# New orders for all engines, and another stretch of late landings in the planner, in an attention and squared-ReLU kernel

## The chip, the core and the metric

The kernel runs on one core of a Trainium2 chip. The metric is the device time of one execution in microseconds: 356.66 us before, the median of three runs (356.45 to 357.16). All times are microseconds (us) unless marked ns. The engines are TensorE (PE, its weight loads PEld), VectorE (DVE), ScalarE (ACT), GpSimd (POOL) and SyncE (SP).

## The reference

Inputs are float32: `q`, `k`, `v` of shape (8 batches, 8 heads, 576 positions, 64), a table of 32 buckets x 8 heads, and two weight matrices.

```python
scores = q @ k.T / 8 + bias_table[bucket(|i - j|)]      # bucket: exact below 16, then logarithmic, 31 from 128 on
attn   = softmax(scores)                                # per batch and head, 576 x 576
x      = (attn @ v), heads put side by side             # 4608 tokens x 512
h      = maximum(x @ w_in, 0)                           # w_in 512 x 2048
out    = (h * h) @ w_out                                # w_out 2048 x 512, float32 result
```

## The kernel before

**Attention.** Two heads make a pair; there are 32 pairs, four to a batch. The softmax is taken without its maximum: the exponential of the scaled scores is multiplied by the exponential of the bias, which is one constant outside a band round the diagonal, so that only the band is multiplied (`tt`, L807, on DVE). The exponential of the table is built at the start: six pieces of 16 small matmuls each on PE (`t_mm`, L531), evacuated by ACT (L543) or DVE (L545).

A pair's q and k are loaded by POOL's queue with a cast to fp16 (L439), into one of five places `qs`/`ks`; for batches 0 and 1 PE transposes them (`tr`, L1096), and ACT (L793) or DVE (L795) copies them out of PSUM into `qt`/`kt`. Later batches are transposed by DMAs that SP issues (L1079). The first pair's q and k come in as float32 by SP and ACT and are cast (L657 on ACT, L659 on DVE). The last 64 keys of both heads share one matmul; for it two small copies per pair put them on a block diagonal in `kz` (L1123, POOL or DVE).

Batch 0 is worked in two halves of its queries (L1013 to L1037), four pairs each. For one pair and half: two score groups of four matmuls (L961), each into two PSUM banks and out through one exponential of 128x1024 on ACT (L1013); one matmul for the last keys (L1028) and its exponential (L1037); band products on DVE; the values (`pv`, L833 and L840) on PE, which need all four value tiles and both tails of the batch; a reciprocal and a product that normalise (L854, L859). Values of batches 0 and 1 are loaded by token tile, one DMA for each 128 tokens (`va`) and two for the last 64 (`vm`). Later pairs have one score group per 128 keys, with an exponential of 128x1024 each (L1143).

**Feed-forward.** Tokens go in nine groups of 512. Group 0 runs its first layer in halves as soon as half of batch 0 is done (L1585; ReLU L1596 on ACT or L1598 on DVE; square L454 on ACT or L456 on DVE). The other first layers (L1633, or L1512 with seven products in place of eight) and second layers (L1342, seven products for eight, with sums of weights L1272 and of activations L1297 on DVE) fill PE between the attention's matmuls from some 54 us to the end.

**What sets the order.** Every operation has a number, counted in the order in which the Python code makes it. `TURNS` (L69) is a table with, for each engine, the numbers in the order in which that engine runs them; where an operation may run on ACT or DVE (or DVE or POOL), the list that holds its number decides. `Plan.schedule` walks these lists with planned durations and planned landings of loads; it doesn't change the order on an engine, but it settles which PSUM bank or buffer an operation takes and how the engines' instructions are interleaved in the program. In it, `SLOW` says between which planned times a DMA lands later, and by how much:

```python
late = SLOW[2] if e == "DMA" and SLOW[0] < at < SLOW[1] else 0.0
```

Of the kernel before, what the change touches and what calls it, by code (L numbers as in the profile page):

```python
# [70 lines left out]
12 15 21 17 19 537 23 535 541 543 25 559 563 571 547 553 573 561 549 555 575 583 587 585 568 597 595 599 580 622  # L71
626 592 604 624 609 607 628 667 669 735 733 637 611 641 683 634 613 652 686 654 639 680 643 656 762 619 658 747
749 677 649 664 760 789 787 814 816 741 739 692 673 671 689 745 820 766 710 707 743 701 770 704 713 768 774 822
716 695 698 719 776 772 755 757 722 756 830 795 782 784 854 858 797 783 675 863 824 867 801 799 793 874 878 803
828 883 887 836 809 826 892 896 811 810 837 838 903 907 841 843 914 847 845 918 952 944 950 851 849 875 942 948
979 871 884 880 911 973 971 977 889 946 864 860 975 855 900 1008 981 1002 893 1004 904 925 1010 958 1000 959 960
1006 1035 987 988 989 922 915 1016 1029 1037 1017 1078 1079 1018 1161 1033 1081 1082 1031 1159 1039 1089 1093
1186 1192 1045 1047 1046 1098 1221 1163 1194 1102 1190 1107 1111 1196 1188 1157 1118 1122 1225 1223 1217 1129
1133 1215 1202 1165 1108 1115 1204 1219 1203 1119 1167 1254 1090 1067 1060 1062 1069 1130 1126 1137 1072 1086
1075 1099 1104 1064 1095 1140 1231 1250 1244 1232 1248 1233 1293 1376 1294 1380 1173 1252 1174 1296 1175 1246  # L80
1372 1297 1304 1401 1378 1260 1308 1261 1262 1313 1374 1407 1382 1317 1322 1403 1432 1440 1326 1333 1438 1436
1430 1337 1434 1344 1388 1409 1348 1405 1389 1390 1446 1585 1591 1448 1447 1587 1305 1593 1411 1583 1341 1319
1352 1589 1417 1459 1277 1275 1419 1418 1282 1279 1301 1284 1463 1334 1330 1645 1290 1310 1465 1651 1461 1287
1345 1314 1641 1467 1469 1323 1355 1649 1599 1600 1601 1504 1505 1475 1670 1672 1477 1476 1507 1508 1674 1515
1678 1614 1519 1524 1528 1680 1647 1618 1533 1537 1643 1612 1657 1544 1545 1534 1676 1548 1566 1616 1541 1488
1659 1486 1493 1658 1490 1555 1556 1498 1525 1495 1521 1622 1854 1563 1856 1501 1552 1530 1512 1516 1559 1628
1686 1620 1687 1688 1715 1716 1827 1630 1629 1718 1719 1802 1800 1862 1726 1730 1852 1860 1823 1735 1739 1744
1796 1804 1794 1748 1755 1798 1759 1727 1858 1810 1825 1766 1741 1697 1699 1811 1704 1763 1706 1812 1732 1701
1709 1770 1883 1889 1887 1712 1777 1752 1891 1829 1831 1774 1767 1868 1881 1833 1723 1736 1870 1756 1885 1869
1745 2044 1839 2038 1840 1841 1930 1931 1897 2075 2046 1898 1933 1899 2048 2073 1934 1941 2077 2009 2011 1945  # L90
1950 2067 2017 2040 1954 1959 2042 2013 1963 2069 2015 2054 1970 1967 2056 2055 1912 2071 1974 1960 1916 1914
2096 2019 1947 1919 2102 2098 1942 1938 2100 1978 2104 2083 1924 1921 2084 1992 1989 1927 2085 1971 1982 1956
2025 2112 2106 2026 1951 2027 2113 2114 2185 2186 1981 1985 2188 2189 2193 2194 2196 2197 2199 2200 2204 2123
2125 2130 2147 2145 2127 2152 2132 2205 2135 2138 2154 2167 2157 2176 2213 2149 2160 2212 2169 2174 2216 2209
2245 2179 2238 2240 2223 2171 2182 2247 2256 2220 2296 2298 2258 2250 2253 2242 2314 2315 2260 2263 2265 2317
2276 2274 2318 2268 2281 2271 2322 2323 2325 2300 2278 2283 2326 2303 2305 2286 2328 2289 2329 2308 2333 2311
# [3 lines left out]
6 2 10 13 52 16 18 20 24 536 544 560 572 564 574 562 550 576 584 588 586 598 596 600 627 623 625 610 629 608 638  # L100
642 612 614 653 655 640 681 644 657 682 659 748 750 679 761 790 817 742 740 672 690 746 821 767 712 744 702 709
771 714 769 823 715 696 775 697 777 773 699 723 700 831 796 859 798 825 868 802 800 794 804 829 827 842 848 953
945 951 943 949 980 885 877 886 974 978 972 947 861 976 856 866 901 982 1009 1005 1003 905 1011 1001 906 927
1007 1036 923 916 1030 1038 1080 1162 1034 1032 1040 1160 1187 1193 1222 1195 1191 1164 1197 1158 1189 1226 1218
1224 1216 1166 1220 1117 1120 1168 1255 1121 1061 1131 1127 1128 1071 1139 1074 1088 1100 1065 1101 1096 1141
1251 1245 1249 1377 1295 1381 1253 1247 1373 1402 1379 1375 1383 1408 1404 1441 1433 1439 1437 1435 1431 1410
1406 1586 1592 1588 1306 1412 1307 1584 1342 1594 1321 1590 1354 1276 1460 1280 1281 1464 1303 1335 1336 1646
1331 1311 1652 1462 1466 1347 1642 1468 1470 1356 1325 1650 1506 1671 1673 1675 1679 1615 1681 1648 1619 1644
1613 1546 1547 1677 1567 1617 1542 1543 1487 1491 1492 1558 1526 1527 1522 1623 1855 1857 1553 1554 1531 1532
# [1633 lines left out]
```

## Time and profile before

| what | value |
|---|---|
| median of three runs | 356.66 us |
| the profiled execution's own time | 356.16 us |
| its span, first to last instruction | 354.2 us |
| PE busy | 346.2 us (98%) |
| DVE, ACT, POOL busy | 304.0, 270.0, 164.4 us |
| mean granted TensorE clock | 0.995 |
| DMA | 44.38 MB, mean 125 GB/s |

The page lists busy time by engine, then the span in 40 slices, DMA queues, the chain of work that ended last, and the costliest groups of instructions. Matmuls are pipelined, so that a busy PE is not PE at its peak. A timeline row gives start, duration, engine, line, operation, written tile, read tile, shape and count, and in brackets the idle time before it with what ended it. A row of waits gives the sum, the number and the longest.

### The profile page before, as it was taken

The numbers are of one execution on the slowest core, as the hardware profiler recorded it, in microseconds if no ns is written. First come the engines' busy times: TensorE is split into PE (matmuls) and PEld (weight loads), VectorE is DVE, ScalarE is ACT, GpSimd is POOL, SyncE is SP. The second block draws the span as 40 slices with busy tenths as digits, with TensorE's granted clock in tenths as the row PEclk, the third lists the DMA queues.
The fourth block names the chain that finished last, engine by engine and source line by source line (L and its number), as shares of the span: only waits on it lengthen the run. The fifth ranks groups of instructions, "written<-read, shape, count | busy, mean of one in ns | idle before, by whom it ended". The sixth has DMA issues, their size and how long they took to land.

```text
span 354.2 us, 10890 instructions
## 1 busy us (share of the span) xinstructions
PE 346.2 (98%) x4456; PEld 259.3 (73%) x4456; DVE 304.0 (86%) x624; ACT 270.0 (76%) x400; POOL 164.4 (46%) x282
## 2 busy tenths in 40 slices
PE   8799999999999999999999999999999999999996
PEld 7577777854687657778776757765777788878885
DVE  5899999779986989787999797789968998999993
ACT  5898996379978788789968684889797941999820
POOL 8857669589969759596856632300000000000000
PEclk9899999999999999999999999999999999999999
DMA  9999999999999999999999978632522042000023
GB/s 170 184 185 174 205 170 144 126 189 175 153 186 165 193 145 143 171 195 171 153 127 172 165 58 150 138 78 67 78 51 78 2 59 89 31 31 32 17 75 120
DMA packets 161378, 44.38 MB, mean 125 GB/s; under 512 B 144688, under 2 KB 161328, under 8 KB 161328
## 3 DMA queue, kind: packets, MB, share of 16 engines
q0 software_dynamic: 74144, 14.53, 50.3%
q1 hardware_dynamic: 86928, 28.86, 47.1%
q8 instruction: 35, 0.57, 0.7%
q10 hardware_dynamic: 256, 0.30, 0.3%
q14 instruction: 15, 0.12, 0.1%
HBM read 36.94 MB, written 9.44 MB: 131 GB/s over the span
## 4 chain that ended last, share of the span: by engine, by line
PE 83%; ACT 8%; DVE 4%; DMA 2%; issue 1%; POOL 1%; ACTq 0%; POOLq 0%
PE bank L1342 32%; PE bank L1633 17%; PE bank L1512 10%; PE bank L899 9%; PE bank L961 7%; ACT pt L1143 3%; DMA ks<-in_k_dram 2%; ACT pt L1013 2%; PE bank L1156 2%; PE bank L968 1%; PE bank L883 1%; PE bank L1585 1%; ACT g L454 1%; PE bank L840 1%; DVE g L456 1%
## 5 line engine op out<-in xcount | busy, mean ns | idle before, releaser
L1143 ACT ACTIVATE pt<-bank 128x1024 f16<-128x1024 f32 x112 | 110.2, 1030 | 13.3 <-PE bank L961 12.9
L1633 PE MATMUL bank<-xt,w_in_sb 128*128 128x512 f16 (+4 forms) x416 | 77.9, 330 | 0.2 <-DVE x L922 0.2
L807 DVE TENSOR_TENSOR pt<-pt,tb_sb 128x512 f16<-128x512 f16 (+3 forms) x108 | 60.5, 574 | 12.9 <-ACT pt L1143 8.6
L439 POOL DMA_DIRECT2D qs<-in_q_dram x79 | 55.8, 712 | 15.2 <-DMA qt<-qs 8.5
L1342 PEld LDWEIGHTS <-g 128*128 128x128 f16 x576 | 54.8, 98 | 8.7 <-issue 2.3
L439 POOL DMA_DIRECT2D ks<-in_k_dram x79 | 55.6, 709 | 2.5 <-issue 1.0
L1633 PEld LDWEIGHTS <-w_in_sb 128*128 128x128 f16 x416 | 36.9, 98 | 26.4 <-issue 3.3
L1342 PEld LDWEIGHTS <-s 128*128 128x128 f16 x432 | 40.8, 98 | 8.5 <-issue 3.6
L961 PE MATMUL bank<-qt,kt 64*128 64x512 f16 (+1 forms) x288 | 42.0, 361 | 0.2
L899 PEld LDWEIGHTS <-pt 128*128 128x128 f16 x1120 | 37.6, 97 | 5.0 <-issue 2.6
L1370 DVE SCALAR_TENSOR_TENSOR y<-bank,y 128x512 f32<-128x512 f32 (+1 forms) x48 | 31.9, 664 | 10.5 <-PE bank L1342 9.8
L899 PE MATMUL bank<-va,pt 128*128 128x65 f16 x1120 | 40.3, 193 | 0.4 <-DVE pt L807 0.4
L1342 PE MATMUL bank<-w_out_sb,s 128*128 128x256 f16 x288 | 36.1, 273 | 0.0
L1342 PE MATMUL bank<-wt,g 128*128 128x256 f16 x288 | 35.9, 273 | 0.0
L1123 POOL COPY kz<-kt 64x64 f16<-64x64 f16 x59 | 18.2, 309 | 37.3 <-DMA kt<-ks 28.2
L1342 PE MATMUL bank<-w_out_sb,g 128*128 128x256 f16 x288 | 35.1, 273 | 0.0
L454 ACT ACTIVATE g<-rt 128x512 f16<-128x512 f16 x49 | 30.9, 639 | 2.0 <-DVE rt L1664 1.4
L1662 ACT ACTIVATE rt<-bank 128x512 f16<-128x512 f32 x42 | 24.8, 596 | 7.6 <-PE bank L1633 7.3
L1664 DVE TENSOR_SCALAR rt<-bank 128x512 f16<-128x512 f32 x38 | 26.0, 687 | 4.2 <-PE bank L1633 3.1
L727 POOL CAST va<-f 128x512 f16<-128x512 f32 x24 | 16.2, 678 | 22.2 <-issue 14.0
L1297 DVE TENSOR_TENSOR s<-g,s 128x1024 f16<-128x1024 f16 x36 | 24.6, 691 | 0.0
L922 DVE TENSOR_TENSOR x<-bank,r 128x640 f16<-128x640 f32 x28 | 22.9, 819 | 0.4
(120 smaller groups left out, 559.8 us busy)
## 6 DMA issues: line engine op xcount, KB each, us to landing
out_dram<-y SPq DMA_DIRECT2D x34, 256.0 KB, 2.4
f<-in_v_dram SPq DMA_DIRECT2D x24, 256.0 KB, 4.8
qs<-in_q_dram POOLq DMA_DIRECT2D x48, 64.0 KB, 4.9
ks<-in_k_dram POOLq DMA_DIRECT2D x48, 64.0 KB, 4.9
w_in_sb<-in_moe_w_in_dram POOLq DMA_DIRECT2D x4, 512.0 KB, 7.1
w_out_sb<-in_moe_w_out_dram POOLq DMA_DIRECT2D x4, 512.0 KB, 10.4
va<-in_v_dram POOLq DMA_DIRECT2D x8, 128.0 KB, 6.5
qs<-in_q_dram POOLq DMA_DIRECT2D x7, 144.0 KB, 6.2
```

The lines of the kernel that those rows point to most:

```text
L439: lambda: io(eng.dma_start(out=out_(), in_=in_())),
L454: io(nc.scalar.activation(out=out_, in_=src, func=SQUAREF))
L807: io(nc.vector.tensor_tensor(out=a, in0=a, in1=t, op=MULT))
L899: nc.tensor.matmul(of_head(st, e)[:, ts(i, 65)], pt[:, c : c + 128], va[:, jt, 2 * hp + e, 0:65], start=False, stop=(jt == 3), skip_group_ ...
L961: nc.tensor.matmul(banks[i][e], kt[rw[e], ts(jt, 128)], qt[rw[e], ds(q0, n)], start=True, stop=True)
L1143: nc.scalar.activation(out=p5(pts[pb.slot])[:, jt, :, 0:512], in_=in_two(st), func=EXPF, scale=SCALE)
L1342: nc.tensor.matmul(home[bf.slot][:, ts(s_, HALF)], left(c, s_), right(c), start=(c == 0 and (s_ == 0 or apart) and (own or i not in before ...
L1370: nc.vector.scalar_tensor_tensor(out=dst, in0=ps, scalar=OSC, in1=ys[y[plus].slot][:, cs], op0=MULT, op1=mybir.AluOpType.add,)
L1512: nc.tensor.matmul(ps()[:, ds(HALF * f + a, z - a)], left()[:, kk, ts(f, 128)], right(a, z)[:, kk, :], start=(first_ and f == 0 and a == 0 ...
L1633: nc.tensor.matmul(g_ps[bank.slot][:, a:z], w_in_sb[:, kk, ts(nt, 128)], xt_sb[:, kk, c : c + z - a], start=(kk == 0), stop=(kk == 3),)
L1662: io(nc.scalar.activation(out=rts[rb.slot], in_=g_ps[bank.slot], func=RELUF))
L1664: io(nc.vector.tensor_scalar_max(out=rts[rb.slot], in0=g_ps[bank.slot], scalar1=0.0))
```

## The change

Two things are edited. `SLOW` goes from 800 ns late between 12.0 and 23.0 us of the plan to 550 ns late between 8.4 and 9.8 us. All five lists of `TURNS` are replaced. The set of operations is the same, and so are their sizes; 133 operations run on another engine than before (most are ReLUs, squares and copies out of PSUM, about as many from ACT to DVE as the other way), and loads stand in another order in POOL's list.

```diff
 TURNS = {
     "PE": """
-12 15 21 17 19 537 23 535 541 543 25 559 563 571 547 553 573 561 549 555 575 583 587 585 568 597 595 599 580 622
+12 15 19 25 23 537 541 535 549 547 559 543 21 587 17 573 563 583 571 575 561 555 553 585 568 595 599 597 580 622
...
     "POOL": """
-53 65 55 73 57 67 71 69 75 59 539 61 63 545 103 77 540 87 99 81 551 79 107 85 97 83 109 89 738 737 111 105 93 95
+53 67 65 55 75 61 69 71 59 57 539 73 551 63 87 545 103 77 81 99 79 107 558 85 109 89 97 737 738 83 105 111 113
...
-SLOW = 12000.0, 23000.0, 800.0
+SLOW = 8400.0, 9800.0, 550.0
```

All line numbers after the table are one lower in the changed kernel, whose table takes one line less. Numbers at the ends of names are places: `qs_70`/`ks_71` hold pair 1, `qs_72`/`ks_73` pair 2, `qs_74`/`ks_75` pair 3, `qs_76`/`ks_77` pair 4; `qt_78` to `qt_81` and `kt_82` to `kt_85` are pairs 0 to 3 of batch 0.

POOL's queue before, from its fourth load on (ahead of it stand the loads of `qs_70`, `qs_72` and `ks_71`):

```order
L439 DMA qs_74<-in_q_dram 96x2x384
L439 DMA va<-in_v_dram 128x8x64
L439 DMA ks_73<-in_k_dram 96x2x384
L439 DMA vm<-in_v_dram 64x4x64 x2
L439 DMA ks_75<-in_k_dram 96x2x384
L439 DMA va<-in_v_dram 128x8x64
L1123 COPY kz<-kt_82 64x64
L439 DMA va<-in_v_dram 128x8x64 x2
L1123 COPY kz<-kt_83 64x64
L439 DMA w_in_sb<-in_moe_w_in_dram 128x4x512
L439 DMA ks_77<-in_k_dram 96x2x384
L1123 COPY kz<-kt_82 64x64
```

POOL's queue now, from its third load on (ahead of it stand the loads of `qs_70` and `ks_73`):

```order
L438 DMA qs_72<-in_q_dram 96x2x384
L438 DMA ks_71<-in_k_dram 96x2x384
L438 DMA ks_75<-in_k_dram 96x2x384
L438 DMA va<-in_v_dram 128x8x64
L438 DMA vm<-in_v_dram 64x4x64 x2
L438 DMA va<-in_v_dram 128x8x64 x2
L1122 COPY kz<-kt_82 64x64
L438 DMA qs_74<-in_q_dram 96x2x384
L1122 COPY kz<-kt_84 64x64
L438 DMA va<-in_v_dram 128x8x64
L438 DMA qs_76<-in_q_dram 96x2x384
L1122 COPY kz<-kt_83 64x64
```

Pair 2's k goes from the sixth to the second place, pair 3's k from the ninth to the fifth, and pair 3's q from the fourth to the eleventh; pair 1's k is fourth instead of third. The second copy for pair 0's block diagonal is no longer on POOL (DVE makes it), and pair 1's copy now stands behind the load of pair 4's q.

ACT's queue before, from the cast of pair 0's k to the exponentials of the first half:

```order
L657 ACTIVATE ks_69<-g_101 96x768
L543 ACTIVATE tb_sb<-bank 128x8x64 x4
L793 ACTIVATE qt_78<-bank 128x576
L793 ACTIVATE kt_83<-bank 128x576
L1013 ACTIVATE pt<-bank 128x2x2x256 x3
L1037 ACTIVATE pm<-bank 128x256 x2
L793 ACTIVATE kt_84<-bank 128x576
L1013 ACTIVATE pt<-bank 128x2x2x256 x3
```

The same stretch of ACT's queue now:

```order
L656 ACTIVATE ks_69<-g_101 96x768
L542 ACTIVATE tb_sb<-bank 128x8x64
L656 ACTIVATE qs_68<-g_101 96x768
L542 ACTIVATE tb_sb<-bank 128x8x64
L792 ACTIVATE qt_79<-bank 128x576
L792 ACTIVATE kt_84<-bank 128x576
L1012 ACTIVATE pt<-bank 128x2x2x256
L792 ACTIVATE kt_83<-bank 128x576
L1012 ACTIVATE pt<-bank 128x2x2x256
L1036 ACTIVATE pm<-bank 128x256
L1012 ACTIVATE pt<-bank 128x2x2x256 x2
```

The cast of pair 0's q comes to ACT (DVE had it), two of the four table pieces leave it, pair 2's k is copied ahead of the first exponential instead of behind the fifth piece of softmax work, and pair 1's k is copied behind the first exponential instead of ahead of it. The second exponential of ACT belongs now to pair 2 and not to pair 1.

On PE the same pieces are reordered to match: before, the scores of pairs 0 and 1 came first and pair 2's k was transposed behind both last-key matmuls; now pair 2's k and q are transposed ahead of all scores, two of the six table pieces stand between the first score groups, and pair 3's transposes, q among them, come behind the scores of pairs 0, 1 and 2.

171 rows, old and new, of the table TURNS are left out of this document.

## Prediction

> **What bounds the kernel now.** I read the page, then the engines by stretches, then PE's waits.
>
> ```profile
> span 354.2 us, 10890 instructions
> ...
> PE 346.2 (98%) x4456; PEld 259.3 (73%) x4456; DVE 304.0 (86%) x624; ACT 270.0 (76%) x400; POOL 164.4 (46%) x282
> ```
>
> PE sets the end. From the table of stretches (time, length, then busy PE, PEld, DVE, ACT, POOL, and the clock):
>
> ```profile
> 22.00:60.00 38.00, 36.72 (x599) 29.18 (x599) 37.02 (x94) 33.91 (x53) 26.91 (x47) 1.00 1.49 172
> 60.00:354.20 294.20, 290.81 (x3516) 216.08 (x3515) 251.29 (x483) 219.34 (x324) 119.63 (x204) 1.00 0.89 115
> ```
>
> From PE's waits (sum, times, longest):
>
> ```profile
> PE bank L1028 <- POOL kz L1123: 1.8, 1, 1.8
> ...
> PE bank L1096 <- issue: 0.7, 1, 0.7
> PE bank L899 <- DVE pt L807: 0.4, 1, 0.4
> PE bank L1633 <- DVE x L922: 0.2, 1, 0.2
> ```
>
> The last row is the only wait behind 60 us. So there PE is a stream of the same matmuls in any order, and a new order can change little in it but the number of turns between kinds of matmul. What is left to win or lose is ahead of 60 us: 1.8 us for one small copy, and what PE loses while ACT makes the exponentials of batch 0's first half. PE after 60 us starts when that is over, so a microsecond there is a microsecond at the end.
>
> How the 1.8 us come about stands in the chain of waits of the first 26 us (start, duration, what):
>
> ```profile
> 4.86 7.01 DMA ks<-in_k_dram
> ...
> 12.15 0.65 POOL ks L439
> ...
> 12.84 0.24 POOL kz L1123
> ```
>
> Pair 2's k, POOL's sixth load, lands at 11.87. POOL's fourteenth load (pair 4's k) is issued 0.28 us later: I read this as eight loads under way at most, the fourteenth waiting for the sixth; the ninth bears it out (below). Pair 0's second `kz` copy stands behind that load, PE behind the copy:
>
> ```profile
> 9.21 1.19 PE L961 MATMUL bank<-qt,kt 64*128 64x256 f16 x12
> ...
> 13.13 0.28 PE L1028 MATMUL bank<-qt,kz 128*128 128x256 f16 x1 [1.79 <-POOL kz L1123]
> ...
> 14.20 1.50 PE L961 MATMUL bank<-qt,kt 64*128 64x256 f16 x12
> ```
>
> and behind PE waits ACT (its timeline):
>
> ```profile
> 9.64 2.85 ACT L1013 ACTIVATE pt<-bank 128x1024 f16<-128x1024 f32 x3 [0.17 <-PE bank L961]
> 12.37 0.40 ACT L1037 ACTIVATE pm<-bank 128x256 f16<-128x256 f32 x1
> 13.45 0.38 ACT L1037 ACTIVATE pm<-bank 128x256 f16<-128x256 f32 x1 [0.67 <-PE bank L1028]
> 13.83 0.65 ACT L793 ACTIVATE kt<-bank 128x576 f16<-128x576 f16 x1
> 14.85 2.85 ACT L1013 ACTIVATE pt<-bank 128x1024 f16<-128x1024 f32 x3 [0.36 <-PE bank L961]
> 17.58 0.68 ACT L1037 ACTIVATE pm<-bank 128x256 f16<-128x256 f32 x2
> 18.11 3.82 ACT L1013 ACTIVATE pt<-bank 128x1024 f16<-128x1024 f32 x4
> ```
>
> From 9.64 to 21.93 ACT makes ten large exponentials, four small ones and one copy, with idle gaps of 0.67 and 0.36 us. It sets the pace here: scores wait for banks that it frees, the first half's values and the feed-forward's first matmuls for its results. The account therefore goes by ACT's stretch.
>
> **The change part by part.** *Loads.* POOL's issue times before, and the landings of q and k pairs and of value tiles (the tile views of `ks`, `qs`, `va` in the first 20 us, in that order):
>
> ```profile
> 2.71 0.66 POOL L439 DMA_DIRECT2D ks<-in_k_dram  x1
> ...
> 7.24 0.65 POOL L439 DMA_DIRECT2D ks<-in_k_dram  x1 [0.43 <-DMA qs<-in_q_dram]
> 7.88 0.91 POOL L439 DMA_DIRECT2D va<-in_v_dram  x1
> ...
> 9.00 1.75 POOL L439 DMA_DIRECT2D va<-in_v_dram  x2
> ```
>
> ```profile
> DMA to landing us min/median/max: 5.6/7.0/7.4
> ```
>
> ```profile
> DMA to landing us min/median/max: 5.5/6.0/7.5
> ```
>
> ```profile
> DMA to landing us min/median/max: 5.1/5.6/7.1
> ```
>
> A q or k load occupies POOL for 0.65 us, a value tile for 0.91, and the ninth waits for the first landing until 7.24. In the new list pair 2's k is second, issued at 2.1 and landed at 7.7 by the shortest row (11.87 before); pair 1's k is fourth, 3.35 + 5.7 = 9.05, some 0.65 later than now. The ninth and tenth loads are value tiles: 7.24 + 2 x 0.91 = 9.06. Then come pair 0's `kz` copy 0.24, pair 3's q 0.65, pair 2's copy 0.24: the last value tile is issued at 10.2, done at 11.1; pair 4's q at 11.75; pair 1's copy at 12.0. That copy is what the next score step of pair 1 waits for.
>
> *The first exponential.* The rows for pair 0's casts and a copy on DVE:
>
> ```profile
> L657 ACT ACTIVATE ks<-g 96x768 f16<-96x768 f32 x1 | 0.8, 843 | 1.6 <-DMA g<-in_k_dram 1.6
> ```
>
> ```profile
> L659 DVE CAST qs<-g 96x768 f16<-96x768 f32 x1 | 0.6, 556 | 0.4 <-DMA g<-in_q_dram 0.4
> ...
> L795 DVE COPY kt<-bank 128x576 f16<-128x576 f16 x2 | 1.5, 752 | 0.6 <-PE bank L1096 0.6
> ```
>
> The cast of q moves to ACT: 0.84 for 0.56, 0.3 us later. Against that, PE's first score group no longer stands behind pair 1's k and a table piece. Cast from 6.78 to 7.62, transposes to 8.1, copy on DVE to 8.9, scores from 8.95, exponential at 9.4: 0.25 us earlier than 9.64. Value taken: -0.25 (bounds -0.45 and 0).
>
> *ACT's stretch.* From 9.4: one exponential, issued each 0.90 us (three in 2.85), the copy of pair 1's k (0.65, was ahead of the stretch; the copy of pair 2's k, 13.83 before, has left it), pair 2's exponential until 11.85. Then the small exponential of pair 1 needs the last-key matmul, which needs POOL's copy of 12.0: matmul 12.0 to 12.3, exponential at 12.3, ACT idle for 0.5. From there scores of three pairs lie ready in the banks, since the transposes of pairs 0, 1 and 2 are done by 9.5. So 1.03 us of gaps go and 0.5 come: -0.53. Bounds: if the copy is held by the wait for a load's place (pair 3's k landing 7.0 after its issue at 4.0, plus 0.3, q's issue 0.65 and the copy: 12.2) the gap is 0.7; if POOL has caught up it is none: -1.03 to -0.33.
>
> *Half clock.* The table of stretches again, columns as above:
>
> ```profile
> 10.26:13.67 3.41, 1.60 (x45) 1.08 (x43) 3.28 (x8) 2.74 (x5) 2.89 (x7) 1.00 2.16 162
> 13.67:17.08 3.41, 3.41 (x50) 2.33 (x44) 2.06 (x8) 3.04 (x5) 3.37 (x6) 0.50 1.31 205
> ```
>
> After 3.41 us with PE busy for 1.60, the clock is 0.50 for 3.41. Twelve score matmuls took 1.50 us there and 1.19 at 9.21. ACT lost by it at most the 0.36 counted above. In the new order PE's gap is from some 10.9 to 12.0, and busy time between 10.26 and 13.67 comes to about 2.2 us (an estimate by the rows' durations); whether this keeps the clock up no row tells. Value 0, bounds 0 and +0.4.
> [...]
>
> *Work moved between DVE and ACT.* From 22 to 60 us DVE is busy for 37.02 of 38, ACT for 33.91, so DVE is nearly a second bound. Its rows there, and ACT's:
>
> ```profile
> L1598 DVE TENSOR_SCALAR rt<-bank 128x512 f16<-128x512 f32 x9 | 6.2, 685 | 0.0
> L456 DVE TENSOR_TENSOR g<-rt 128x512 f16<-128x512 f16 x9 | 4.0, 453 | 0.0
> ```
>
> ```profile
> L454 ACT ACTIVATE g<-rt 128x512 f16<-128x512 f16 x7 | 4.6, 656 | 0.2 <-DVE rt L1598 0.2
> ```
>
> By the lists DVE has 7 of these ReLUs instead of 9 and 11 squares instead of 9, two 576-column copies fewer and one smaller copy fewer: -1.4 + 0.9 - 1.5 - 0.4 = -2.4 us. ACT gains some 1.8 and has 4 us free. It can win at most PE's 0.4 us of waiting for DVE (L899 above). I take half: -0.2, bounds -0.4 and 0.
>
> *Turns of PE.* A group of sixteen matmuls costs 0.10 more when the kind of matmul changes (chain of waits):
>
> ```profile
> 97.09 1.75 PE bank L1342 x16
> ...
> 111.54 1.85 PE bank L1342 x16
> ```
>
> Counted in the two lists there are 147 such turns before and 148 now: +0.1. The 0.7 us "issue" wait of L1096 I leave: nothing in the profile says what ends it.
>
> *Sum.* -0.25 - 0.53 + 0 - 0.2 + 0.1 = -0.88. Behind 60 us nothing is taken off or added: the same matmuls, PE waiting 0.2 us, and `out` stores still hang on the last matmul. The profiled execution took 356.16 us, of which 1.96 lie outside its span; it is 0.50 below the median of the runs. By its own time the changed kernel takes 355.28; put on the median, 356.66 - 0.88 = **355.8 us**. The bounds added up give -1.8 to +0.2 (354.9 to 356.8).
>
> **Rivals.** *1. The gain stops at DVE.* From 22 to 60 us DVE's work decides. If it can't start earlier, because its copies of pair 4 wait for k and q whose loads are now issued later (pair 4's k at 12.7 to 12.9 behind the first w_in, 12.15 before), or because the new list puts work ahead of what PE needs, then PE merely waits there. For it: 37.02 of 38. Against it: DVE has 2.4 us less to do, and it waited for ACT before 22 us (2.06 busy of 3.41). Time: between no gain and a third of it, 356.4.
>
> *2. Slower: the last value tile.* PE's list has the first values of pair 0 ahead of pair 3's scores, and they need all value tiles. The last tile is issued at 10.2. With the shortest landing, 5.1, it is there at 15.3; ACT wants pair 3's scores at 12.3 + 0.33 + 0.9 x 4 + 0.32 x 2 = 16.9, values take 0.7 and scores 0.25, so nothing is lost up to a landing of 15.8. With the longest of the row, 7.1, it lands at 17.3; the values take 1.11 at half clock (15.82 to 16.93 in PE's timeline below), and ACT stands until 18.7: +1.8 us.
>
> ```profile
> 15.82 0.32 PE L833 MATMUL bank<-vm,pm 128*128 128x130 f16 x1
> ...
> 16.93 0.34 PE L1028 MATMUL bank<-qt,kz 128*128 128x256 f16 x1
> ```
>
> From a landing of 6.5 us after issue (16.7) the 0.88 are gone, beyond it the kernel is slower; at the end of the row 356.66 - 0.88 + 1.8 = 357.6. For it: pair 3's q is now loaded just ahead of that tile, and the page's sixth load took 7.01. Against it: the same twelve loads lie up to this tile as before, so the same bytes have to pass, and the last tile was issued only 0.3 us earlier in the old order (9.00 + 0.87).
>
> *3. The change does less than it says.* `SLOW` alters no order, and the lists could be good only for planned landings. If pair 1's k lands at 10.3 (7.0 after issue), PE, ACT and the copy stall for it, the gap is 1.0 instead of 0.5 and the first exponentials lose their 0.25: 356.5. I count this with rival 1 as no change.
>
> **How the numbers follow.** The forecast 355.8 gets 0.44, rivals 1 and 3 together 0.38 (356.4 to 356.5), rival 2 0.18 (357.6). A measurement of this kernel tells a difference of about 0.2%, 0.7 us, from none: faster is below 355.95, slower above 357.37. The forecast lies just inside faster, so its chance is shared: faster 0.43, within 0.2% 0.40, slower 0.17. For the range I take the forecast's lower bound of 354.9, moved to 355.0 since not all bounds meet, and rival 2's 357.6 at the top.
>
> **What would show it.** Right: PE's wait at L1028 for `kz` shrinks from 1.8 to about 1 us and ends near 12.0; ACT's gaps between the first large exponential and 21 us add up to some 0.5 us; the tenth large exponential ends near 21.0 instead of 21.93; the first feed-forward matmul (L1584 there) starts some 0.8 us earlier; behind 60 us PE still waits for next to nothing. Wrong: ACT waiting at 16 to 19 us for pair 3's scores, with PE behind a `va` landing (rival 2); the front earlier but a new PE wait for DVE or for `issue` between 24 and 60 us (rival 1); a `kz` wait that ends after 12.5; or waits behind 60 us that the old order did not have, which would make the whole argument, that only the front counts, wrong.

## The result and the profile after

The changed kernel takes **354.62 us** (median of nine executions, 353.70 to 355.80) against 356.68 us for nine of the kernel before: a ratio of 0.9947, interval 0.9931 to 0.9964, or 1.9 us less (1.3 to 2.5). In a later series the ratio was 0.9929 (0.9903 to 0.9956). The forecast was 355.8 with a range from 355.0: the direction was right, the gain more than twice as large. The profiled execution took 354.8 us, 1.8 of them outside its span.

From the page of the changed kernel:

```profile
span 353.0 us, 10901 instructions
...
PE 344.6 (98%) x4456; PEld 259.6 (74%) x4456; DVE 303.1 (86%) x621; ACT 268.7 (76%) x397; POOL 167.8 (48%) x286
```

Its front did nearly what was forecast. ACT's timeline, and PE's round the `kz` wait and at the first feed-forward matmul (lines lie one lower than before):

```profile
9.94 1.02 ACT L1012 ACTIVATE pt<-bank 128x1024 f16<-128x1024 f32 x1 [0.15 <-PE bank L960]
10.86 0.64 ACT L792 ACTIVATE kt<-bank 128x576 f16<-128x576 f16 x1
...
18.08 2.94 ACT L1012 ACTIVATE pt<-bank 128x1024 f16<-128x1024 f32 x3
```

```profile
12.11 0.27 PE L1027 MATMUL bank<-qt,kz 128*128 128x256 f16 x1 [0.52 <-DVE kz L1122]
...
23.46 0.94 PE L1584 MATMUL bank<-xt,w_in_sb 128*128 128x256 f16 x7
```

The `kz` wait ends at 12.11 (forecast 12.0), the tenth large exponential at 18.08 + 2.94 = 21.02 (21.0; before 21.93), and the first feed-forward matmul starts 0.91 us earlier than its row before:

```profile
24.37 0.83 PE L1585 MATMUL bank<-xt,w_in_sb 128*128 128x256 f16 x6
```

In these two executions none of this is left at 35 us. Both kernels stop in the same place of PE's program, among the transposes for batch 1; first the kernel before, then the changed one:

```profile
34.24 0.25 PE L1096 MATMUL bank<-id_sb,ks 96*64 96x96 f16 x4
35.20 0.36 PE L1096 MATMUL bank<-id_sb,ks 96*64 96x96 f16 x8 [0.71 <-issue]
```

```profile
33.67 0.25 PE L1095 MATMUL bank<-id_sb,qs 96*64 96x96 f16 x3
35.36 0.63 PE L1095 MATMUL bank<-id_sb,qs 96*64 96x96 f16 x21 [1.44 <-issue]
```

PE comes to the stop earlier, and in these two executions it leaves it at 35.20 and 35.36 us. The "issue" wait, which the forecast had left out of the sum, grew from 0.71 to 1.44 us. That is not so in every execution. In a second profiled execution of the changed kernel PE goes on at 34.55:

```profile
34.55 0.63 PE L1095 MATMUL bank<-id_sb,qs 96*64 96x96 f16 x21 [0.66 <-issue]
```

Matched matmul by matmul, the two executions of the changed kernel lie within 0.03 us of each other from 18 to 33 us, 0.81 us apart behind the stop and 0.95 at the end, so what this stop takes or leaves is still there at the end. What the first of them wins for good against the kernel before, it wins behind 35 us. The table of stretches (time, length, then busy PE, PEld, DVE, ACT, POOL, the clock, DMA) of the kernel before, then of the changed one:

```profile
50.00:60.00 10.00, 9.57 (x161) 7.73 (x156) 10.00 (x22) 7.16 (x13) 9.85 (x16) 1.00 1.68 141
80.00:100.00 20.00, 19.78 (x257) 11.70 (x256) 19.30 (x40) 18.38 (x28) 19.55 (x34) 1.00 1.70 162
```

```profile
50.00:60.00 10.00, 10.00 (x165) 8.43 (x164) 9.77 (x23) 7.49 (x14) 8.02 (x11) 1.00 0.88 77
80.00:100.00 20.00, 20.00 (x262) 12.77 (x261) 19.78 (x41) 17.77 (x27) 19.55 (x31) 1.00 1.67 161
```

PE's idle 0.43 and 0.22 us are gone there; one new wait, of 0.29 us for a ReLU, stands at 77 us. To see more than idle time, I added up for each stretch what PE's operations took beyond the usual spacing of their kind (the 20% quantile over six kernels' traces). Taken so, the changed kernel leads by 0.6 us at 22 us, by 0.0 at 35, by 0.1 at 50, by 0.9 at 60, by 0.8 at 100 and by 1.2 at the end, which is the difference of the spans.

### The profile page after: what moved, and what is told of

Same layout as the page of the kernel before. It is cut to its first block, busy times and chain, and to the rows that moved or that the text cites. A ratio compares the mean times of both kernels' runs of the same rounds, so it can differ in the third digit from the quotient of the medians.

```text
span 353.0 us, 10901 instructions
## 1 busy us (share of the span) xinstructions
PE 344.6 (98%) x4456; PEld 259.6 (74%) x4456; DVE 303.1 (86%) x621; ACT 268.7 (76%) x397; POOL 167.8 (48%) x286
## 4 chain that ended last, share of the span: by engine, by line
PE 93%; DVE 4%; DMA 1%; issue 1%; ACT 1%; SPq 0%; DVEq 0%
PE bank L1341 32%; PE bank L1632 20%; PE bank L1511 10%; PE bank L898 10%; PE bank L960 8%; PE bank L1584 4%; PE bank L1155 2%; PE bank L882 2%; PE bank L967 1%; DVE pt L806 1%; PE bank L1095 1%; DMA g<-c_oh 1%; PE bank L839 1%; PE bank L1215 1%; DVE qt L794 1%
## 5 line engine op out<-in xcount | busy, mean ns | idle before, releaser
L806 DVE TENSOR_TENSOR pt<-pt,tb_sb 128x512 f16<-128x512 f16 (+3 forms) x108 | 62.1, 585 | 12.3 <-ACT pt L1142 10.7
L960 PE MATMUL bank<-qt,kt 64*128 64x512 f16 (+1 forms) x288 | 40.7, 356 | 0.6 <-ACT pt L1012 0.3
L1122 POOL COPY kz<-kt 64x64 f16<-64x64 f16 x59 | 20.0, 339 | 31.9 <-DMA kt<-ks 25.3
L1663 DVE TENSOR_SCALAR rt<-bank 128x512 f16<-128x512 f32 x41 | 27.8, 685 | 6.9 <-PE bank L1632 6.0
L453 ACT ACTIVATE g<-rt 128x512 f16<-128x512 f16 x46 | 29.1, 640 | 3.0 <-DVE rt L1663 2.5
L1661 ACT ACTIVATE rt<-bank 128x512 f16<-128x512 f32 x39 | 22.8, 598 | 8.2 <-PE bank L1632 7.3
L726 POOL CAST va<-f 128x512 f16<-128x512 f32 x24 | 18.2, 769 | 21.9 <-PE bank L898 10.7
L1296 DVE TENSOR_TENSOR s<-g,s 128x1024 f16<-128x1024 f16 x36 | 24.6, 696 | 0.0
L921 DVE TENSOR_TENSOR x<-bank,r 128x640 f16<-128x640 f32 x28 | 22.8, 815 | 0.2
```

Source lines behind the costliest of these rows:

```text
L453: io(nc.scalar.activation(out=out_, in_=src, func=SQUAREF))
L806: io(nc.vector.tensor_tensor(out=a, in0=a, in1=t, op=MULT))
L960: nc.tensor.matmul(banks[i][e], kt[rw[e], ts(jt, 128)], qt[rw[e], ds(q0, n)], start=True, stop=True)
L1296: io(nc.vector.tensor_tensor(out=out_, in0=a, in1=b_, op=mybir.AluOpType.subtract))
L1663: io(nc.vector.tensor_scalar_max(out=rts[rb.slot], in0=g_ps[bank.slot], scalar1=0.0))
```

## The experiments

Theory A is the prediction's: the gain is made ahead of 23 us. Its rivals came out of the two traces: something between 22 and 100 us, where DVE is busy for 72.0 of 78 us in the kernel before, makes it; and the "issue" stop takes the front's gain away. All times below are medians beside executions of the kernel before on the same chip (356.9 to 357.2 us).

### The front alone

**One copy earlier.** In POOL's list of the kernel before, pair 0's second `kz` copy (540) is moved ahead of two loads:

```diff
-... 539 61 63 545 103 77 540 87 99 ...
+... 539 61 63 545 540 103 77 87 99 ...
```

> The kernel before with one number moved: pair 0's second kz copy stands in POOL's queue ahead of the loads of w_in and of pair 4's k, so that it no longer waits for a load's place. If only the wait counts (ACT's gap of 0.67 us goes, pair 2's k still lands at 11.9): about 0.7 us faster, 356.0, with the clock as before. If the half clock that follows PE's gap counts too: PE is idle for some 0.6 us instead of 1.79, the clock stays up, and the time comes to about 355.0. If the front doesn't matter at all: 356.7.

It took 358.18 us, ratio 1.0035 (1.0020 to 1.0051): slower. The 1.8 us wait at 13.1 us is gone, and another of 1.45 us came behind it, for another pair's copy; and 80 us later there is a wait that the old order did not have. Rows of PE, then DVE, of this kernel:

```profile
15.87 0.28 PE L1028 MATMUL bank<-qt,kz 128*128 128x256 f16 x1 [1.45 <-POOL kz L1123]
...
93.10 0.31 PE L883 MATMUL bank<-vm,pm 64*128 64x65 f16 x9 [1.03 <-DVE x L922]
```

```profile
92.23 0.81 DVE L922 TENSOR_TENSOR x<-bank,r 128x640 f16<-128x640 f32 x1
```

PE's order is the same as before, but the planner, which settles banks by walking the lists with its own times, now gave these matmuls the bank from which DVE still makes `x`. So a list that is edited at 12 us moves a wait at 92 us. Matched with the kernel before, PE is 0.45 us ahead at 80 us and 0.75 us behind at 100: the slower time speaks of the banks, not of the copy.

**PE's gap filled.** 26 idle matmuls, which `KEEP` adds, stand in the kernel before where PE waits at 11 us (`KEEP = [26]`), meant to keep the clock up:

> The kernel before with 26 idle 128x128 matmuls on zeros (52 instructions more on PE) in PE's gap of 1.79 us, so that the wait stays and the clock has a busy PE to go by. If the half clock costs what the prediction said (nothing, at most 0.4): 356.4 to 356.8. If the half clock is where the gain beyond the forecast went: mean clock 1.0 instead of 0.995 and about 355.5. If the fillers themselves delay PE: 356.8 to 357.2.

357.64 us, ratio 1.0029 (1.0012 to 1.0046). In the profiled execution the clock stayed up (mean granted clock 1.000, 0.995 in the kernel before), and the first feed-forward matmul came at 23.83 us, 0.54 us earlier than in the kernel before, whose granted clock was 0.50 from 13.7 to 17.1 us:

```profile
23.83 0.94 PE L1585 MATMUL bank<-xt,w_in_sb 128*128 128x256 f16 x7
```

So of the 0.91 us by which the changed kernel's row led, some 0.5 may be the half clock of that one execution of the kernel before, and not the order. What the clock is worth at the end this run can't tell, since the waits (sum, times, longest) show the same change of banks, and a longer wait at 52 us:

```profile
PE bank L883 <- DVE x L922: 1.1, 1, 1.1
...
PE bank L899 <- DVE pt L807: 0.9, 1, 0.9
```

**The changed kernel, filled** (`KEEP = [8, 5, 4]`, three gaps of PE before 15 us):

> The changed kernel with 8, 5 and 4 idle matmuls in its three small gaps of PE near 11.6, 13.5 and 14.5 us. Three of its nine runs have a mean clock of 0.99 and take 355.4 to 355.8, six have 1.0 and take 353.7 to 354.8. If those gaps bring the half clock on: all runs at 1.0 and a median of about 354.3. If not: the same split, 354.6. Because 34 instructions are added, the instruction fetch wait of L1095 may move.

355.40 us, ratio 0.9957 (0.9937 to 0.9976): no better than the changed kernel alone. With 34 more instructions ahead of it the "issue" stop no longer appears among its waits, but the fillers cost the front more than a microsecond (by PE's spacing, 1.4 us at 25 us).

**The changed order up to 23 us only**, the old order behind it (`TURNS` of the changed kernel for the operations that start before 23 us of the plan, then those of the old one):

> The changed kernel's orders for everything that starts ahead of 23 us in the plan, then the orders of before (SLOW as before). If the front holds the whole gain: 354.6. If the front gives the 0.9 us that were forecast and the rest comes from 22 to 60 us: 355.8, and a wait of PE for DVE at L899 near 52 us as before.

356.80 us, ratio **1.0003** (0.9987 to 1.0019). Its profiled execution has the new front (its `kz` wait is 0.6 us, the first feed-forward matmul comes 0.8 us earlier than before), then the stop for "issue", and at 52 us a wait of 0.60 us that was 0.43 before:

```profile
34.35 0.37 PE L1096 MATMUL bank<-id_sb,ks 96*64 96x96 f16 x9 [0.67 <-issue]
...
52.92 0.75 PE L899 MATMUL bank<-va,pt 128*128 128x65 f16 x19 [0.60 <-DVE pt L807]
```

The stop takes nothing here: matched with the kernel before, PE is 0.80 us ahead at 30 us, 0.84 at 36, 0.50 behind the wait at 52 us and 0.49 at the end. But this was the fastest of twelve executions. By all twelve theory A falls: the front alone is worth at most 0.5 us at the end (the interval), and next to nothing by the median.

### The rest alone

**The old order up to 23 us, the changed one behind it**:

> The complement of the kernel that had the changed order only up to 23 us: here the old order up to 23 us, the changed order behind it. Theory 'front' (the prediction): the gain is made before 23 us, so hardly anything is left here, 356.7. Theory 'behind the front': the gain is made by the order behind 23 us, 355.0, and PE's wait for op 779's pt at 52 us (0.6 us in the old order) is gone, although the kz wait of 1.8 us at 12 us is still there.

355.22 us, ratio **0.9954** (0.9938 to 0.9970), with the old front. Most of the gain lies behind 23 us. The `kz` wait of 1.8 us, though, is not in its profiled execution. PE's matmuls ran at a low clock there, PE came to pair 0's two last-key matmuls later, and they run without a wait, two in 0.73 us (in the kernel before one took 0.28 at a granted clock of 1.00, 0.40 at 0.50):

```profile
13.03 0.73 PE L1027 MATMUL bank<-qt,kz 128*128 128x256 f16 x2
```

In five profiled executions with the old front and a low clock at the start, PE waits for that copy not at all in three, and 0.26 and 0.60 us in the others. The 1.8 us belong to the one execution that the forecast read.

**The changed order up to 60 us, the old one behind it**:

> The changed order up to 60 us, the old one behind it. If the stretch from 22 to 60 us makes the gain (where DVE is busy for 35 to 37 of 38 us), about 355.0. If it is made behind 60 us, where PE is a stream, about 356.5; then waits of PE between 60 and 100 us should be there as in the old kernel (0.2 to 0.4 us at 93 us).

359.30 us, ratio 1.0060 (1.0038 to 1.0082). This does not tell the two stretches apart: at the seam the planner again gave PE a bank that waits for `x`, 1.6 us at 92 us (`PE bank L882 <- DVE x L921`, the first row of its waits). It shows only that the old order behind 60 us is not safe from DVE.

**One product earlier on DVE**, in the kernel before:

```diff
-717 526 720 718 780 721 531 779 532 724 ...
+717 526 720 718 780 721 779 531 532 724 ...
```

> The old kernel with one move: on DVE the product of pair 5's largest block with its table (pt, L807, op 779) goes one place forward, ahead of one sum of w_out pieces (wt, L1272). PE's values of pair 5 waited 0.6 us for it at 52.8 us. If that wait is what holds the old kernel in this stretch, the wait is gone and the time falls by 0.5 to 0.6 us, to 356.3. If DVE as a whole is the limit there, another wait takes its place and the time stays at 356.9.

357.47 us, ratio 1.0015 (1.0001 to 1.0029), with two waits of PE for DVE that the kernel before did not have, 0.46 us at 60 us and 0.35 at 91. The product (779, the row of 1536 columns) did not come earlier. Rows of DVE, POOL and PE of this kernel:

```profile
51.77 0.84 DVE L456 TENSOR_TENSOR g<-rt 128x512 f16<-128x512 f16 x1
52.54 0.94 DVE L807 TENSOR_TENSOR pt<-pt,tb_sb 128x1536 f16<-128x1536 f16 x1
```

```profile
51.68 0.65 POOL L727 CAST va<-f 128x512 f16<-128x512 f32 x1
```

```profile
53.54 0.75 PE L899 MATMUL bank<-va,pt 128*128 128x65 f16 x19 [0.34 <-DVE pt L807]
```

The square ahead of it took 0.84 us where its kind takes 0.42; in the kernel before it was the sum of `w_out` pieces, then ahead of it, that took 0.83. What is long in either is not one operation, but what overlaps a cast on POOL.

### The casts on POOL

Values of batches 2 and later come as float32 into `f` and are cast to `va` by POOL (L727). The kernel before, at 50 us: DVE, POOL, PE.

```profile
50.24 0.77 DVE L456 TENSOR_TENSOR g<-rt 128x512 f16<-128x512 f16 x1
...
51.68 0.83 DVE L1272 TENSOR_TENSOR wt<-w_out_sb 128x512 f16<-128x512 f16 x1
52.43 0.95 DVE L807 TENSOR_TENSOR pt<-pt,tb_sb 128x1536 f16<-128x1536 f16 x1
```

```profile
50.08 0.65 POOL L727 CAST va<-f 128x512 f16<-128x512 f32 x1
...
51.37 0.85 POOL L727 CAST va<-f 128x512 f16<-128x512 f32 x1
```

```profile
53.43 0.75 PE L899 MATMUL bank<-va,pt 128*128 128x65 f16 x19 [0.43 <-DVE pt L807]
```

Each of these two DVE products starts inside a cast and ends 0.28 to 0.29 us after it (cast 50.08 + 0.65 = 50.73, product 51.01; cast 51.37 + 0.85 = 52.22, product 52.51). Together they put off the 1536-column product by 0.8 us, and PE waits for that. Two DVE products are long beside the casts of 86.0 and 87.3 us too, ahead of the `x` of 92 us: a sum of 0.91 us that ends 0.54 us after the first cast and a square of 1.00 us that ends 0.29 us after the second. What holds the products the rows don't say; whether it is the casts, the next run asks. The forecast had not looked at them.

**Four casts cut** in the kernel before:

```diff
-lambda room=room, dst=dst: io(nc.gpsimd.tensor_copy(out=dst(), in_=room())),
+lambda room=room, dst=dst, cut=(b, tt) in ((2, 0), (2, 1), (3, 1), (3, 2)): io(
+    nc.gpsimd.tensor_copy(out=dst()[:, 0:1, 0:8], in_=room()[:, 0:1, 0:8])
+    if cut else nc.gpsimd.tensor_copy(out=dst(), in_=room())
+),
```

This kernel leaves four value tiles unfilled but for 8 columns, so its output is not the reference's; it serves for its time alone.

> The old kernel, in which four of GpSimd's casts of value tiles (va<-f, L727: batch 2's first two, at 50.1 and 51.4 us, and batch 3's second and third, at 86.0 and 87.3 us) cast 8 columns instead of 512; so 4 of 10 tiles of those batches aren't filled and the output there is not the reference's. In the old trace the DVE instruction that overlaps such a cast takes 0.4 to 0.6 us longer than its kind, and op 779's pt, for which PE waits 0.6 us at 52.8 us, stands behind two of them. Theory 'casts': these instructions go back to their usual length, 779 ends at 52.6 instead of 53.4 us, PE's wait there and the one at 59.4 us (0.3) shrink, the wait at 93 us too: 0.6 to 1.2 us less, 355.7 to 356.3. Theory 'order': DVE is late by its order alone and the time stays at 356.9, or falls by under 0.3 us.

356.02 us, ratio **0.9969** (0.9951 to 0.9987), and in the last series 355.48 us, ratio 0.9955 (0.9940 to 0.9969): 1.1 and 1.6 us less. Rows of DVE and PE for the places above:

```profile
50.13 0.42 DVE L456 TENSOR_TENSOR g<-rt 128x512 f16<-128x512 f16 x1
...
51.28 0.42 DVE L1275 TENSOR_TENSOR wt<-w_out_sb 128x512 f16<-128x512 f16 x1
51.62 0.95 DVE L810 TENSOR_TENSOR pt<-pt,tb_sb 128x1536 f16<-128x1536 f16 x1
```

```profile
52.72 0.78 PE L902 MATMUL bank<-va,pt 128*128 128x65 f16 x20
```

Both products are back at 0.42 us, the large one is done at 52.57 and PE doesn't wait. Matched with the kernel before, whose PE order it has, each of the two profiled executions of this kernel gains 0.6 us at 53 us, 0.2 at 59 and 0.4 at 93, and loses 0.1 at two or three places: 0.8 and 1.0 us in all.

**The same cut in the changed kernel**:

> The same cut of the same four casts in the changed kernel, where they run at 56.1, 57.6, 82.6 and 83.2 us and PE waits for nothing near them. Theory 'casts' (the changed order has moved them off the products that PE waits for): no gain here, 354.6, within 0.3. Theory 'order': if the cut helps as much here as in the old kernel, it says nothing about the difference between the two.

354.54 us, ratio 0.9932 (0.9914 to 0.9951), the changed kernel's own time (354.62 and 354.45), as far as an interval of 0.7 us either way can tell. In its order the two casts of batch 2 stand at 56.1 us and the product is made by 51.7; DVE and POOL of the changed kernel:

```profile
50.36 1.36 DVE L806 TENSOR_TENSOR pt<-pt,tb_sb 128x1536 f16<-128x1536 f16 x2
```

```profile
56.05 2.12 POOL L726 CAST va<-f 128x512 f16<-128x512 f32 x2
```

There the cast gives way: the two take 2.12 us (0.65 and 0.85 in the kernel before), and the two products that overlap the first keep 0.42 us each. So four casts cost the old order 1.1 to 1.6 us and the new one nothing that can be seen. That is about half of what the change brings (1.9 to 2.7 us).

### The stop for "issue", and the clock at the start

The chip's DMA rows have a queue for instructions; for the changed kernel, as for the one before:

```profile
q8 instruction: 35, 0.57, 0.7%
```

35 transfers of 16 KB for 8912 weight loads and matmuls are some 255 instructions each. Counted in the traces, PE stops at its instruction 1210 or 1211 in the old kernel, in the changed one and in the front alone, and from 88 us on fetches begin just after instructions 2491, 2747 and 3003, which lie whole multiples of 256 behind it. There a fetch begins 0.3 to 1.5 us after the block ahead of it is entered; in the first 50 us it is 1.0 to 4.4 us in these three traces (POOL's loads, q0, take 123% of the DMA engines' span there in the kernel before and 129% in the changed one; what delays a fetch is not shown). In the changed kernel the fetch begins at 33.09 and PE goes on at 35.36; in the old one at 32.75 and 35.20, in the front alone at 31.91 and 34.35, in the second execution of the changed kernel at 32.31 and 34.55. In all twelve traces with this stop PE goes on 2.2 to 2.5 us after the fetch begins. The fetch begins 3.1 to 3.8 us after PE entered the block ahead in eleven of them, and 4.4 us after in the first of the changed kernel. So an earlier front mostly has an earlier fetch; why that one was late no trace shows.

**Other blocks.** In the changed kernel, 76 idle matmuls of 44 columns stand in place of 26 of 128 ahead of 5 us:

```diff
-CLOCK = 17, 9
+CLOCK = 50, 26
...
-g_ps[far_b.slot + bank][:, 0:128], idle_sb, idle_sb, start=True, stop=True
+g_ps[far_b.slot + bank][:, 0:44], idle_sb, idle_sb[:, 0:44], start=True, stop=True
```

> The changed kernel with 50 additional idle matmuls in the first 5 us, where PE waits for data anyway (76 of 44 columns for 26 of 128), so that the boundary of a block of 256 PE instructions, at which PE stood for 1.65 us at 33.7 us while the next block was fetched, falls on other work, some 100 instructions earlier in the program. Theory 'fetch': the stall falls from 1.65 to under 0.3 us; if DVE's work between 40 and 60 us allows it, the time falls by 1.0 to 1.4 us, to 353.2 to 353.6; if DVE takes it back at 50 us, PE's waits there grow and it stays at 354.6. Theory 'no fetch': the issue stall stays where it is in the program, 1.65 us at the transposes, and the time at 354.6.

355.10 us, ratio 0.9944 (0.9922 to 0.9967). The stop is gone; the transposes of 33.67 run through, later:

```profile
35.24 0.45 PE L1095 MATMUL bank<-id_sb,ks 96*64 96x96 f16 x12
35.52 0.68 PE L1095 MATMUL bank<-id_sb,qs 96*64 96x96 f16 x24
```

That alone would not settle what "issue" was, since PE comes there only at 35.24 us: its clock was low until 16 us (sixteen score matmuls took 1.89 us at 13.59, 1.16 in the changed kernel), and it was 1.9 us behind the changed kernel at 30 us. The missing stop gave 1.6 of that back, and the time did not fall. The next two kernels settle the cause.

**The gap ahead of 5 us filled** (`CLOCK = 17, 14`), and **both** (`CLOCK = 50, 26` with 58 columns), meant to have the clock up sooner:

> The changed kernel with 5 more idle matmuls of 128 columns ahead of 5 us, where PE stood idle for 0.5 to 1.2 us and waited for a table (0.6 us of PE time). In the profiles so far PE's clock reached full speed at 8.6 to 10 us in three executions of the new front, and only at 14 to 16 us in two others, whose exponentials then ran 0.5 to 1.8 us later. Theory 'clock': the gap ahead of 5 us breaks the busy stretch that raises the clock; filled, the clock is up by 10 us in nearly every run, and the runs lie closer together, with a median near the lower end of the changed kernel's range (353.7 to 355.8): 354.0. Theory 'no': same median, 354.6 to 355, same spread of 2 us.

> Both: 76 idle matmuls of 58 columns instead of 26 of 128, which fill PE until 5.2 us and move the boundary of the instruction blocks as in the kernel with 44 columns, where the fetch stall of 1.65 us at 34 us was gone, but PE's clock stayed low until 16 us. If the clock is up by 10 us here, front and fetch add up: PE is some 0.9 us ahead of the changed kernel at 60 us, 353.5 to 353.8. If a gain ahead of 40 us is taken back by DVE between 40 and 60 us, 354.6.

355.29 us (ratio 0.9944, 0.9921 to 0.9966) and 355.69 us (0.9962, 0.9944 to 0.9981): neither is better than the changed kernel, and their executions still spread by 1.4 and 2.5 us. PE's stops for "issue", of the first, then of the second:

```profile
34.37 0.40 PE L1095 MATMUL bank<-id_sb,ks 96*64 96x96 f16 x10
35.16 0.23 PE L1095 MATMUL bank<-id_sb,ks 96*64 96x96 f16 x2 [0.39 <-issue]
```

```profile
11.32 0.47 PE L530 MATMUL bank<-eb_sb,g 128*128 128x32 f16 x11 [1.27 <-issue]
```

With 10 more instructions the stop stands at the same count, 1211, and so two matmuls ahead of the end of the `ks` transposes instead of three matmuls into `qs`. With 100 more the boundary ahead falls on table matmuls at 10 us; the fetch begins at 8.87 and PE goes on 2.45 us later. So the "issue" waits are the boundaries of blocks, and moving one can bring another. In the second kernel the clock was up from 4.3 us, fell to half at 11.1, at the end of that stop, and rose again at 14.5. No version beat the changed kernel.

### What the front is worth

Four kernels on one chip: the changed one, the old front with the new rest, and the old rest with the four casts cut, with the new front and with the old one.

> The changed kernel once more, as the measure for the next three on one chip: 354.6.

> The old order up to 23 us and the changed one behind it, once more, beside the changed kernel. Theory 'front carries where the rest lets it': the changed front is worth its 0.6 to 0.8 us here, so this kernel takes 0.6 to 0.8 us more than the changed one, 355.3. Theory 'front is worth nothing': the two agree within 0.3 us.

> The changed order up to 23 us, the old one behind it, with the four casts cut as before (4 of 10 value tiles of two batches aren't filled). With the casts in place this front gained nothing that could be measured. Theory 'front carries where the rest lets it': with the collisions gone it takes 0.5 to 0.8 us less than the old kernel with the same cut (356.0): 355.3. Theory 'front is worth nothing': 356.0, as without it.

> The old kernel with the four casts cut, once more, beside the run above: 356.0, 1.0 us under the old kernel.

| front | rest | median us | ratio to before |
|---|---|---|---|
| new | new | 354.45 | 0.9929 (0.9903 to 0.9956) |
| old | new | 354.91 | 0.9940 (0.9917 to 0.9962) |
| new | old, casts cut | 356.48 | 0.9977 (0.9961 to 0.9994) |
| old | old, casts cut | 355.48 | 0.9955 (0.9940 to 0.9969) |

Ahead of the new rest the new front is 0.5 us better, less than the intervals can tell; ahead of the old one with the casts cut it is 1.0 us worse, and with the casts in place it made no difference (1.0003). The third kernel's profiled execution shows how that can be. PE and ACT of the changed kernel repeated, then of the third kernel:

```profile
9.43 0.39 PE L960 MATMUL bank<-qt,kt 64*128 64x256 f16 x4
...
12.28 1.16 PE L960 MATMUL bank<-qt,kt 64*128 64x256 f16 x16
```

```profile
18.04 2.94 ACT L1012 ACTIVATE pt<-bank 128x1024 f16<-128x1024 f32 x3
```

```profile
9.89 0.61 PE L964 MATMUL bank<-qt,kt 64*128 64x256 f16 x4
...
13.05 1.89 PE L964 MATMUL bank<-qt,kt 64*128 64x256 f16 x16
```

```profile
19.78 2.87 ACT L1016 ACTIVATE pt<-bank 128x1024 f16<-128x1024 f32 x3
...
22.49 0.81 ACT L1040 ACTIVATE pm<-bank 128x320 f16<-128x320 f32 x2
```

The same sixteen score matmuls take 1.89 us instead of 1.16: PE ran at a low clock until 15 us, and each of them took 390 to 417 ns, as score matmuls of the kernel before did where its granted clock was 0.50 (a median of 414 ns from 14.2 to 15.3 us, against 269 from 9.2 to 10.1 us at 1.00). The new front has few gaps for that to hide in: its tenth large exponential starts at 21.6 us there, at 19.8 to 19.9 in the two executions of the changed kernel, and the first feed-forward matmul at 25.09 instead of 23.46. The old front has its first feed-forward matmul at 24.0 to 25.0 us in five executions with a low clock at the start, at 24.37 where the clock was up until 13.7 us, and at 23.83 where it stayed up. So the new front leads the kernel before by 0.6 to 0.9 us where the clock is up by 10 us (23.43 to 23.77 in four executions without added matmuls), leads the filled old front by 0.1 to 0.4, and leads not at all, or trails, where the clock is low (24.6 and 25.1 in two).

In six of ten profiled executions with the new front the clock was up by 10 us and stayed up. Of the timed ones only a mean clock is kept, which misses a low start (it is 1.0 for the third kernel's profiled execution); but the three of nine executions of the changed kernel with a mean of 0.989 or 0.990 are its three slowest, 355.4 to 355.8 us against 353.7 to 354.8. That the clock makes the medians of the table is argued, not shown, and it is not all: the third kernel's profiled execution is 0.6 us behind the fourth's at 30 us and 1.5 at the end, most of the rest lost ahead of score matmuls at 81 and 96 us.

## Where the prediction held and where it failed

**The front.** The sum of the first exponential and ACT's stretch, -0.25 - 0.53 = -0.78, came out as -0.91 at the tenth exponential, but not by its parts, and the agreement is partly luck: the first exponential came at 9.94, 0.3 us later and not 0.25 earlier, and of ACT's gaps none of the 0.5 us stayed. Some 0.5 of the 0.91 may be the half clock of the one execution that was read. The `kz` wait and the first feed-forward matmul came as worked out. Rival 2 did not happen: ACT has no gap at 16 to 19 us for pair 3's scores.

**The step that failed** is where the sum looked for the gain: "What is left to win or lose is ahead of 60 us: 1.8 us for one small copy, and what PE loses while ACT makes the exponentials of batch 0's first half", with -0.78 for the front and -0.2 for the work moved between DVE and ACT. The runs put it the other way round: the front alone measured 1.0003, nothing, and the order behind 23 us alone 0.9954 and 0.9940, -1.7 and -2.3 us between the medians. That the sum came out with the right sign is no merit of its main term.

**The term that was mis-sized** is "Work moved between DVE and ACT": -0.2, with -0.4 as its end, because only PE's listed wait could be won. The larger part of what the order behind 23 us brings is not the 2.4 us of work that move from DVE to ACT, but casts on POOL that lengthen DVE's products. It was there in a row that the forecast quoted: nine squares of mean 453 ns and, in the changed kernel's view, eleven of 419. A mean over nine that is 34 ns high is one instruction of 770 ns among eight of 415; eight sums of `w_out` with 468 in place of 418 are the other. Those two stood right ahead of the product for which PE waits. Cutting the casts that lengthen them, with two more at 86 us, took 1.1 to 1.6 us off the old kernel and none that can be seen off the new one.

**"A microsecond there is a microsecond at the end"** failed in the medians, but why is only partly shown. The front's lead did go through in some profiled executions: the second execution of the changed kernel is 1.4 us ahead of the old front with the new rest at 25 us and 1.8 at the end, and the front alone kept 0.49 of 0.80 us ahead of the old rest, where the wait for DVE at 52 us took 0.3. The 0.7 us "issue" wait, which the forecast left aside, is a fetch that comes with PE for the most part, but its delay differs between executions by more than a microsecond (3.1 to 4.4 us). How these things, and the clock at the start, add up to no gain in the median stays open.

**"Behind 60 us PE is a stream"** was wrong too: the one row of 0.2 us there, PE's wait for `x` at 93 us, was a wait with almost no margin. It became 1.0 to 1.6 us in three kernels whose banks fell otherwise, and it is gone in the changed one. What would have shown the step wrong, "waits behind 60 us that the old order did not have", appeared in those three.

**The half clock**, 0 with +0.4 as its bound, looked right in the first trace, where the clock stayed up. Over executions it is larger: with one and the same front the first feed-forward matmul came at 23.57 and 25.09 us, 1.5 us apart, and the loss lies before 15 us and not behind the gap. The clock was up from 8.6 us in the one execution and from 15.0 us in the other; what sets that time no run shows. The 1.5 us are nearly as much as the whole change.

**Turns of PE** (+0.1) are too small to be seen in any of these runs. **Rival 1**'s sign, a longer wait for "issue" or DVE between 24 and 60 us, appeared in the first trace (1.44 us for 0.71) and in the front alone (0.60 for 0.43), but for the change as a whole the rival was wrong, since the new order took the old DVE wait away. The late landing of **rival 3** did not come: the `kz` wait ended at 12.11.

What stays open: what the change brings beyond the casts, 1.0 to 1.5 us where the old kernel with the cut ran beside the changed one, is given to no single cause. PE's spacing puts 0.4 of it behind 100 us in the first trace, and the front may hold 0.5. Whether the work moved from DVE to ACT has a share, no run separates.

## What to carry to other kernels

A wait of 0.2 or 0.4 us in front of a nearly full engine was here not a price of 0.2 or 0.4 us but the visible end of a queue: look at the single instructions that stand ahead of it, one by one, for any that take longer than their kind, and at what GpSimd does in those moments. A wait at a kernel's start that one profiled execution shows may be that execution's own: profile a second one before it is priced. Before a gain in a kernel's first microseconds is carried to its end, walk through the next places where PE stops, and ask of each whether it ends at a time of its own or moves along, as the fetch here mostly did. And where a planner settles buffers, an edit at one place can move a wait at quite another; compare the waits of the whole kernel before reading a slower time as evidence against the edit.

## What the runs showed of the hardware

- PE's instructions came in blocks of 256 (35 transfers of 16 KB), and PE stood when the next was late: 0.4 to 1.4 us at 34 us in twelve traces, where small matmuls use up a block in 5 us (a fetch that starts 3.1 to 4.4 us after its block was entered, and PE going on 2.2 to 2.5 us after it starts). Moving the boundary by 100 instructions removed that stop in two kernels and brought one of 1.27 us at 10 us in one of them.
- Four DVE products of 512 columns that started inside a GpSimd cast (50.24 and 51.68 us of the kernel before, 50.67 and 51.77 us of the one with the product moved) ended 0.28 or 0.29 us after that cast and took 0.77 to 0.84 us; with the casts cut, the products in the first two places took 0.42. At 56 us of the changed kernel it is the cast that took longer, 1.56 us, and the two products that started inside it took 0.42 each.
- The column of the granted clock reads 1.00 where there is no record yet (the first one of this execution is at 15.0 us). The table of stretches of the kernel with the new front and the casts cut, for a stretch in which score matmuls took 390 to 417 ns, as at a granted 0.50 above:

```profile
10.20:13.60 3.40, 3.40 (x59) 2.18 (x57) 3.02 (x6) 2.86 (x4) 3.27 (x7) 1.00 2.03 156
```
